# Early token loads, paired norms by log and exp, idle products and due times in an S4 and mixer kernel

## The chip, the cores and the metric

The kernel runs on one core of a Trainium2 chip. The metric is the device time of one execution in microseconds (us).

## The reference

The input `u` holds 2048 tokens of 512 features in f32. With xn = layernorm(u), the output is u + s * silu(b):

- `s` is an S4 layer: a convolution of every feature over the tokens with a kernel K of 2048 taps, plus xn * Dskip. K(d, l) is the real part of the sum over 128 states of C * dt * B * exp(dt * A * l). The convolution is computed by FFTs of length 4096.
- `b` is a mixer block with a norm of its own: x1 = xn + shift(gelu(layernorm(xn) @ w1)) @ w2, where the four quarters of the features are shifted by +1, -1, +2 and -2 tokens, and b = x1 + gelu(layernorm(x1) @ w3) @ w4, with 1376 hidden features.

```python
def _layernorm(x, axis=-1, eps=1e-5):
    m = jnp.mean(x, axis=axis, keepdims=True)
    v = jnp.var(x, axis=axis, keepdims=True)
    return (x - m) / jnp.sqrt(v + eps)
...
    x = A_u
    xn = _layernorm(x, axis=-1)
    s = _A_ref(xn, A_A_re, A_A_im, A_B_re, A_B_im, A_C_re, A_C_im, A_log_dt, A_Dskip)
    g = _silu(_B_ref(xn, B_w1, B_w2, B_w3, B_w4))
    return x + s * g
```

## The kernel before

**Tokens.** The 2048 tokens lie in the tile `X` as 16 steps of 128 tokens (the partitions) by 512 features. `loads()` brings everything in over the one DMA queue of SyncE (SP). `ln_first(q)` norms four steps at a time: statistics (`bn_stats`, `bn_aggr`) on VectorE (DVE), then `rstd`, a Sqrt on ScalarE (ACT) and a reciprocal on DVE, twice one after the other: `r1` for xn, and `r2` for the norm of xn, whose variance follows from `r1`. `h_pair(j)` transposes two normed steps on TensorE (PE) with `ident` (x2 to the bank pd, copied to `xT`), multiplies by w1 (bank pb) and takes the Gelu on ACT into `hT`. `u_stage1` multiplies the same steps by `ks1`, the first stage of the FFT (bank pa, copied to `ue` and written to the scratch `scr_Ud`).

**Shifts and second product.** `wrapped(k)` copies the shifted columns that cross a step into `hw` on DVE. `hs_pair` multiplies `hT` and `hw` by w2, adds into X and takes statistics. `ln_second` norms all 16 steps at once. `prep(jp)` splits w3 and w4 into two f16 halves each (`w3h`, `w4h`; a scale is a power of two that `pow2_scale` finds through a square root). `mlp(g)`, g from 0 to 7, computes two steps in f16 with three products for each (`x1T` by `w3h`, Gelu, `ghl` by `w4h`).

**The S4 kernel.** `params()` turns A, B, C and dt into logarithms, phases and magnitudes (`pn`, `tm`, then `par`). `tables(hf)` makes tables for eight chunks of 32 features, sixteen chunks `cc` in all: `block` the magnitudes `mag` for two chunks (64 exponentials of 128x64 on ACT, in groups of 16), `phases` and `remainders` the phases on DVE, `waves` the sines on ACT, `sums` the products of magnitudes and waves on DVE (`kt`, `pt`). PE contracts them over the states (bank pc, groups of 64 products for each chunk). `kstage1`, `products` (`uin`, `kin`, `pr`, `z1e`, through the scratch), `inverse` and `finish` are the FFT of the kernel, the product of spectra and the inverse; `gate` is the silu.

**The order.** No operation is issued where it is written. All are recorded by `Plan`, one list for PE, ACT, DVE and SP, and `Plan.order()` then runs a list scheduler over them: an engine takes, of the operations that are ready by the planner's own costs, the one with the least due time. The functions set this by `due(t)`, from constants (`H0`, `HC` for the tokens, `T0`, `TC` for the tables, `M0`, `MC` for the mixer and so on). An ACT function of another table than the loaded one (`TABLES`) adds `SWITCH` to the due time. An operation that may run on ACT or DVE (`E.copy`, `E.affine`) gets `PREFER` on DVE and `AVOID` on ACT:

```python
                    v = o.vt
                    if e == "ACT" and o.table and o.table != table:
                        v += SWITCH
                    if len(o.alts) > 1:
                        v += PREFER if e == "DVE" else AVOID
```

The order on every engine is thus fixed when the program is built; on the chip the engines run through their lists and wait for each other by semaphores. As all is issued from one place, every instruction of the profile has the line L279, and is told apart by its tiles. In the lists of before, the queue brings the tokens of steps 0 to 3 in two parts, the parameters between them, then w1, the other tokens and w2.

Of the kernel before, what the change touches and what calls it, by code (L numbers as in the profile page):

```python
# [83 lines left out]
class Op:  # L84
    __slots__ = (
        "eng", "alts", "calls", "cost", "deps", "succ", "table", "vt", "idx", "nbytes", "n", "ready", "start",
        "alias", "first", "last",
    )


TABLES = {
    AF.Exp: 1, AF.Sin: 2, AF.Arctan: 2, AF.Gelu_apprx_tanh: 3, AF.Sqrt: 4, AF.Silu: 5,
}
LATENCY = {"PE": 0.23, "ACT": 0.16, "DVE": 0.13, "SP": 0.0}
SAME = {"PE": 0.0, "ACT": 0.13, "DVE": 0.1, "SP": 0.0}
TABLE_LOAD = 1.41
DMA_RATE = 300e3
LAND, PAD = 3.32, 0.17
BASE, FINE, END = 16512, 19840, 229368

KGC = 3.25
SWITCH = 135.33
PREFER, AVOID = 290.89, 121.33
PV, T0, TC = 366.3, -80.6, 92.61
M0, MC, WC = 302.7, 225.43, 0.24
H0, HC, SC = -1212.9, 183.55, 0.09
KA, PA, PAC, FA = -108.1, -1278.7, 0.07, 1091.5
KB, PB, PBC, FB = -40.0, -299.0, 0.06, 186.2
FC = 0.16


def mlp_due(g, jp):
# [3 lines left out]
class Plan:  # L116
    def __init__(self, nc):
        self.engines = {"PE": nc.tensor, "ACT": nc.scalar, "DVE": nc.vector, "SP": nc.sync}
        self.ops = []
        self.cells = {}  # L120
        self.vt = 0.0
        self.group = None


# [33 lines left out]

    def new(self, table=0, nbytes=0):
        op = Op()  # L160
        op.alts, op.table, op.nbytes = {}, table, nbytes
        op.deps, op.alias, op.vt, op.idx = set(), set(), self.vt, len(self.ops)
        self.ops.append(op)
        return op


    def add(self, alts, writes, reads, table=0, nbytes=0):
        op = self.group or self.new(table, nbytes)
        for e, (cost, call) in alts.items():
            old = op.alts.setdefault(e, [0.0, []])  # L170
            old[0] += cost
            old[1].append(call)


        def after(other, name):
            if other[0] is not op:
                op.deps.add(other[0].idx)
                if other[1] != name:
                    op.alias.add(other[0].idx)

        for ap in reads:
            me = (op, ap.tensor.name)
            for c in self.cover(ap):
                if isinstance(c, str):
                    op.deps.update(self.cells[c])
                    continue
                st = self.cells.setdefault(c, [None, {}])
                if st[0] is not None:
                    after(st[0], me[1])
                if c[1] == "bank":  # L190
                    for r in st[1].values():
                        after(r, me[1])
                    st[0], st[1] = me, {}
                else:
                    st[1][op.idx] = me
        for ap in writes:
            me = (op, ap.tensor.name)
            for c in self.cover(ap):
                if isinstance(c, str):
                    self.cells.setdefault(c, []).append(op.idx)  # L200
                    continue
                st = self.cells.setdefault(c, [None, {}])
                if st[0] is not None:
                    after(st[0], me[1])
                for r in st[1].values():
                    after(r, me[1])
                st[0], st[1] = me, {}
# [12 lines left out]
    def order(self):  # L220
# [17 lines left out]
        while len(out) < len(ops):  # L238
# [4 lines left out]
            for o in pools[e]:  # L243
                if o.ready <= t + 0.02:
                    v = o.vt
                    if e == "ACT" and o.table and o.table != table:
                        v += SWITCH
                    if len(o.alts) > 1:
                        v += PREFER if e == "DVE" else AVOID
                    if pick is None or (v, o.idx) < score:  # L250
                        pick, score = o, (v, o.idx)
            for k in pick.alts:
# [136 lines left out]
def kernel(  # L389
# [54 lines left out]
    stats = keep([P, S, 6], "stats")  # L444
    mv = keep([P, S, 2], "mv")
    rs = keep([P, 4, S], "rs")
    bs = keep([P, S], "bs")
    wsc = keep([P, 16], "wsc")
    ssq = keep([P, 16], "ssq")
    ks1 = keep([P, 2 * NG], "ks1")  # L450
# [79 lines left out]
        turn["t"] += 1  # L530
        return bank[3][turn["t"] % 2]

    def rstd(dst, var):
        A.activation(dst, var, AF.Sqrt, bias=epst[:, 0:1], scale=1.0)
        V.reciprocal(dst, dst)

    def due(t):
        plan.vt = t


    def by_r(sb, dr, to_dram=False):
# [15 lines left out]
    raw = {"Ar": rawA[:, 0], "Ai": rawA[:, 1], "Br": rawC[:, 0], "Bi": rawC[:, 1], "Cr": rawC[:, 2], "Ci": rawC[:, 3]}  # L557

    def loads():
        due(0)  # L560
        by_r(X[:, 0:2], xv[:, :, 0:2])
        Q.dma_start(ev, c_ev)
        for n, src in (("Br", B_re), ("Cr", C_re), ("Bi", B_im), ("Ci", C_im), ("Ar", A_re), ("Ai", A_im)):
            Q.dma_start(raw[n], src.rearrange("(r p) n -> p r n", p=P))
        Q.dma_start(ld, log_dt.rearrange("(r p) -> p r", p=P))
        by_r(X[:, 2:4], xv[:, :, 2:4])
        load_w(w1, w1s, stile)
        Q.dma_start(ks1, c_ks1)
        for s0 in (4, 8, 12):
            by_r(X[:, s0 : s0 + 4], xv[:, :, s0 : s0 + 4])  # L570
        load_w(w2, w2s, w2place)
        Q.dma_start(is2, c_is2)
        V.memset(Dt, 0.0)
        for r in range(4):
            Q.dma_start(
                Dt[32 * r : 32 * r + 1], Dskip.rearrange("(h r m) -> r h m", h=2, r=4)[r].unsqueeze(0)
            )
# [58 lines left out]
    def block(blk):  # L636
# [23 lines left out]
            wmr[:, q0 : q0 + BQ].unsqueeze(1).to_broadcast([P, 4, BQ]),  # L660
        )
        for i in range(0, L2, 16):
            with plan.together(table=TABLES[AF.Exp]):
                for row in range(i, i + 16):
                    A.activation(mag[:, row], lgr[:, q0 : q0 + BQ], AF.Exp, scale=float(row))
        blocks[blk] = EB, pab, mag

    def phases(cc):

        if cc * CQ % BQ == 0:  # L670
            block(cc * CQ // BQ)
        EB, pab, mag = blocks[cc * CQ // BQ]
        q = cc * CQ
        sl = slice(q % BQ, q % BQ + CQ)
# [58 lines left out]

    def tables(hf):
        for cc in range(8 * hf, 8 * hf + 8):
            due(T0 + TC * cc)
            phases(cc)
            remainders(cc)
            waves(cc)
            sums(cc, factors(cc))  # L740


# [146 lines left out]
    def pow2_scale(cols, dst_s, dst_inv, target):  # L889
# [6 lines left out]
        A.activation(m1, m1, AF.Sqrt)  # L896
# [53 lines left out]
        w4t.append(w)  # L950


    def ln_first(q):
        ss = slice(4 * q, 4 * q + 4)
        for s in range(4 * q, 4 * q + 4):
            V.bn_stats(stats[:, s], X[:, s])
            V.bn_aggr(mv[:, s], stats[:, s])
        r1, r2, v = rs[:, 0, ss], rs[:, 1, ss], rs[:, 2, ss]
        rstd(r1, mv[:, ss, 1])
        V.tensor_mul(v, r1, r1)  # L960
        V.tensor_mul(v, v, mv[:, ss, 1])
        rstd(r2, v)
        V.scalar_tensor_tensor(bs[:, ss], mv[:, ss, 0], -1.0, r1, op0=ALU.mult, op1=ALU.mult)
        for s in range(4 * q, 4 * q + 4):
            E.affine(X[:, s], X[:, s], rs[:, 0, s : s + 1], bs[:, s : s + 1])

    hT = []

    def h_pair(j):
# [3 lines left out]
        for i in range(2):  # L973
            s = 2 * j + i
            x2 = wtile([P, D], F32, "x2")
            E.affine(x2, X[:, s], rs[:, 1, s : s + 1])
# [49 lines left out]
    def hs_pair(s0, k):  # L1026
# [11 lines left out]
        for i in range(2):  # L1038
            s = s0 + i
            V.tensor_add(X[:, s], X[:, s], acc[i])  # L1040
            V.bn_stats(stats[:, s], X[:, s])
            V.bn_aggr(mv[:, s], stats[:, s])

    def ln_second(ss):
        r3 = rs[:, 3, ss]
        rstd(r3, mv[:, ss, 1])
        V.tensor_scalar(r3, r3, XS, None, op0=ALU.mult)
        V.scalar_tensor_tensor(bs[:, ss], mv[:, ss, 0], -1.0, r3, op0=ALU.mult, op1=ALU.mult)


    x1Ts = {}
# [1 line left out]
    def mlp_input(g):  # L1053
# [3 lines left out]
        for i in range(2):  # L1057
            s = 2 * g + i
            xn = wtile([P, D], F32, "x1n")
            E.affine(xn, X[:, s], rs[:, 3, s : s + 1], bs[:, s : s + 1])  # L1060
            pt = t_bank() if g < 2 else mm_bank()
            with plan.together():
                for k in range(4):
# [48 lines left out]

    def token_mixing():
        V.memset(ssq, 0.0)
        for q in range(4):
            due(H0 + 2 * q * HC)
            ln_first(q)
            for j in (2 * q, 2 * q + 1):
                due(H0 + j * HC)
                h_pair(j)  # L1120
                u_stage1(2 * j)
                if j == 0:
                    for k in range(3, 6):
                        wrapped(k)
        for k in range(3):
            wrapped(k)
        for i in range(12):
            due(H0 + 2 * HC + i * 4.0)
            weight_squares(i)
        weight_scales()  # L1130
        due(H0 + 8 * HC)
# [65 lines left out]
```

## Time and profile before

| | |
|---|---|
| median of 3 runs | 680.08 us (679.99 to 680.60) |
| profiled execution | 679.28 us, its span 677.5 us |
| TensorE clock granted, mean | 0.981 |
| ACT table loads | 75, 96.2 us |
| DMA moved | 95.60 MB |

The span is the time between the first and the last instruction of the profiled execution; 1.78 us lie around it. Engines are PE (TensorE products), PEld (its weight loads, which run beside products), DVE, ACT, POOL and SP. A busy PE includes time in which a product is queued in the engine. A row of the timeline gives the start, the duration, the engine, the line, the operation, output<-input with the tiles' names, partitions x elements and count, and in brackets the idle time ahead of it and what ended that.

### The profile page before, as it was taken

The page shows a single profiled execution, that of the slowest core. Times are in us where ns is not written, and L with a number is a line of the kernel's source. Part 1 is how long each engine was busy: PE and PEld are TensorE (multiplying, and loading weights), DVE is VectorE, ACT ScalarE, POOL GpSimd, SP SyncE. Part 2 cuts the span into 40 slices and gives each one's busy share as a digit, 9 for nine tenths or more (in the row PEclk, how much of TensorE's full clock was granted, in tenths as well). Part 3 has the DMA queues.
Part 4 walks back from the last instruction along what each step waited for, and adds up shares of the span by engine and source line. Part 5 has one row for each costly group of instructions (what it writes and reads, how often), then busy time and mean ns, then how long its engine had stood idle before and what let it go on. Part 6 is the DMA issues. An engine that isn't in the chain of part 4 may idle for free.

```text
span 677.5 us, 13618 instructions
## 1 busy us (share of the span) xinstructions
PE 624.4 (92%) x5446; PEld 408.0 (60%) x5446; DVE 547.8 (81%) x783; ACT 459.2 (68%) x1020; POOL 0.7 (0%) x6
## 2 busy tenths in 40 slices
PE   0799999999996989899999999999999999999983
PEld 0376767666455667446768668657665756657541
DVE  4989789999999999999999989996344356465546
ACT  2889699998837999979989789883145342233220
POOL 0000000000000000000000000000000000000000
PEclk9999999899998999999999999999999999999995
DMA  9954442310111201365523342427389936642997
GB/s 245 247 196 141 150 158 102 98 71 20 66 63 49 78 33 48 70 159 155 155 72 110 102 122 83 140 74 196 104 239 346 255 89 193 163 149 78 263 333 229
DMA packets 100751, 95.60 MB, mean 141 GB/s; under 512 B 48656, under 2 KB 81424, under 8 KB 99792
## 3 DMA queue, kind: packets, MB, share of 16 engines
q1 hardware_dynamic: 100688, 94.73, 49.3%
q8 instruction: 43, 0.70, 0.4%
q14 instruction: 20, 0.16, 0.1%
HBM read 61.16 MB, written 33.55 MB: 140 GB/s over the span
## 4 chain that ended last, share of the span: by engine, by line
PE 46%; DVE 39%; ACT 6%; issue 5%; DMA 2%; SPq 1%; ACTq 0%
PE pb L279 16%; PE pa L279 13%; DVE pt L279 11%; PE pd L279 9%; DVE kt L279 8%; PE pc L279 7%; DVE X L279 4%; DVE pab L279 2%; DVE eg L279 2%; DVE stats L279 2%; ACT mag L279 2%; ACT L279 2%; DMA X<-in_A_u_dram 1%; DVE w4h L279 1%; DVE pr L279 1%
## 5 line engine op out<-in xcount | busy, mean ns | idle before, releaser
L279 PE MATMUL pa<-w4h,ghl 128*128 128x512 f16 (+1 forms) x528 | 123.9, 380 | 6.5 <-DVE ghl L279 5.6
L279 PE MATMUL pb<-x1T,w3h 128*128 128x256 f16 (+1 forms) x1056 | 124.2, 273 | 1.4 <-DVE x1T L279 1.2
L279 PEld LDWEIGHTS <-w3h 128*128 128x128 f16 (+1 forms) x1056 | 102.2, 100 | 27.9 <-issue 14.0
L279 ACT ACT_TABLE_LOAD x75 | 96.2, 1283 | 6.4 <-DMA wst<-in_B_w_dram 5.1
L279 PEld LDWEIGHTS <-ghl 128*128 128x128 f16 (+1 forms) x528 | 48.3, 98 | 74.8 <-issue 12.1
L279 ACT ACTIVATE mag<-par 128x64 f32<-128x64 f32 x512 | 83.8, 270 | 5.5 <-DVE kt L279 4.2
L279 PE MATMUL pc<-kt 128*32 128x64 f32 x1024 | 84.2, 416 | 2.7 <-DVE kev L279 1.4
L279 PE MATMUL pc<-pt 128*32 128x64 f32 x1024 | 78.1, 388 | 4.0 <-DVE pt L279 4.0
L279 ACT ACTIVATE g<-pb,wsc 128x512 f32<-128x512 f32 (+1 forms) x48 | 32.6, 690 | 64.0 <-PE pb L279 63.8
L279 PE MATMUL pb<-xT,w 128*128 128x256 f32 x256 | 59.8, 394 | 1.5 <-DVE xT L279 1.0
L279 PEld LDWEIGHTS pc<-pt 128*32 128x32 f32 x1024 | 56.3, 195 | 4.3 <-DVE pt L279 4.3
L279 PEld LDWEIGHTS pb<-xT,w 128*128 128x128 f32 x256 | 49.8, 197 | 14.8 <-DVE wsc L279 1.8
L279 PEld LDWEIGHTS pc<-kt 128*32 128x32 f32 x1024 | 48.6, 177 | 12.5 <-issue 9.5
L279 DVE SCALAR_TENSOR_TENSOR ghl<-g,wsc,ghl 128x512 f16<-128x512 f32 (+1 forms) x48 | 35.1, 744 | 23.8 <-ACT ghl L279 23.8
L279 DVE TENSOR_TENSOR pr<-pd,kh 128x512 f32<-128x512 f32 x48 | 33.6, 726 | 15.6 <-PE pd L279 15.3
L279 DVE TENSOR_TENSOR kt<-mag,kt 128x1024 f32<-128x1024 f32 x32 | 42.4, 1324 | 0.0
L279 DVE SCALAR_TENSOR_TENSOR pt<-kt,pt 128x2080 f32<-128x2080 f32 x16 | 38.9, 2429 | 0.8 <-ACT kt L279 0.7
L279 ACT ACTIVATE kt<-kt,halfpi 128x2080 f32<-128x2080 f32 x16 | 33.1, 2067 | 0.0
L279 ACT ACTIVATE pt<-pt 128x2080 f32<-128x2080 f32 x16 | 31.6, 1973 | 0.1
L279 ACT ACTIVATE ghl<-g,wsc 128x512 f16<-128x512 f32 (+1 forms) x43 | 30.6, 724 | 1.6 <-ACT g L279 0.9
L279 DVE BATCH_NORM_STATS2 stats<-X 128x6 f32<-128x512 f32 x32 | 22.0, 705 | 8.0 <-DMA X<-in_A_u_dram 7.5
L279 PE MATMUL pa<-w,hT 128*128 128x512 f32 x58 | 26.5, 597 | 0.0
(158 smaller groups left out, 920.7 us busy)
## 6 DMA issues: line engine op xcount, KB each, us to landing
wst<-in_B_w_dram SPq DMA_DIRECT2D x20, 512.0 KB, 3.9
scr_Ud<-ue SPq DMA_DIRECT2D x16, 512.0 KB, 3.2
scr_Kfa<-k1e SPq DMA_DIRECT2D x16, 256.0 KB, 3.8
uin<-scr_Ud SPq DMA_DIRECT2D x32, 128.0 KB, 3.1
cst<-c_gp SPq DMA_DIRECT2D x16, 256.0 KB, 2.8
kin<-scr_Kfa SPq DMA_DIRECT2D x32, 128.0 KB, 2.8
scr_Zda<-z1e SPq DMA_DIRECT2D x16, 256.0 KB, 2.7
xr<-in_A_u_dram SPq DMA_DIRECT2D x16, 256.0 KB, 7.6
```

Of the source, the lines that this page charges most:

```text
L279: ins = [getattr(self.engines[op.eng], name)(*args, **kw).ins for name, args, kw in op.calls]
```

## The change

- `loads()`: the queue's order has due times of its own (`LX`, `LC`, `LW`, `LP`, `LV`): the first tokens, w1 and `ks1`, the other tokens, then the parameters, w2 last.
- `rstd`: 1/sqrt(var + eps) is exp(-0.5 * ln(var + eps)) on ACT, and one Newton step of four small operations on DVE. `Ln` has the planner's table number of `Exp`. `pow2_scale` takes its square root by Ln and Exp as well.
- `ln_first`: both norms of a step are one call of `rstd` on a pair of variances (the second from var / (var + eps)), in slices of 2, 2, 4, 4 and 4 steps rather than four of 4.
- 36 products of `ident` by `ident` into a bank that nothing reads stand at the start, and an Exp on a column (`warm`).
- Each call of `due` is a stage of its own, to whose due time an entry of the list `SHIFT` (240 numbers) is added. Groups of magnitudes, phases and sums of one chunk have each their own.
- Operations that read PSUM get `PREFERP` and `AVOIDP` in place of `PREFER` and `AVOID`. All constants of due times are others, as are the planner's `LAND` (time of a DMA to land) and `PAD`.

```diff
-    AF.Exp: 1, AF.Sin: 2, AF.Arctan: 2, AF.Gelu_apprx_tanh: 3, AF.Sqrt: 4, AF.Silu: 5,
+    AF.Exp: 1, AF.Ln: 1, AF.Sin: 2, AF.Arctan: 2, AF.Gelu_apprx_tanh: 3, AF.Sqrt: 4, AF.Silu: 5,
...
-LAND, PAD = 3.32, 0.17
+LAND, PAD = 2.66, 0.13
...
-SWITCH = 135.33
-PREFER, AVOID = 290.89, 121.33
-PV, T0, TC = 366.3, -80.6, 92.61
-M0, MC, WC = 302.7, 225.43, 0.24
-H0, HC, SC = -1212.9, 183.55, 0.09
-KA, PA, PAC, FA = -108.1, -1278.7, 0.07, 1091.5
-KB, PB, PBC, FB = -40.0, -299.0, 0.06, 186.2
-FC = 0.16
+WARM = 36
+
+SHIFT = (
+    -3715, -2638, -688, 1005, -3173, -190, 267, 1280, 1181, 867, -512, -1077, 1355, 105, 2148, 920, 1539, 1545,
...
+)
+Q0, QC = 955.2, 0.12
+SWITCH = 4853.54
+PREFERP, AVOIDP = 3416.47, 1294.57
+PREFER, AVOID = 736.27, 6918.58
+PV, T0, TC = 1461.1, -148.8, 918.24
+LX, LC, LP, LW, LV = -4000.0, 0.11, -3268.4, -5077.4, -2984.5
+M0, MC, WC = 1956.5, 2587.23, 0.2
+H0, HC, SC = -1313.8, 567.49, 0.11
+KA, PA, PAC, FA = 775.7, -1535.4, 0.35, 1765.8
+KB, PB, PBC, FB = 1877.3, -190.5, 0.06, -1173.5
+FC = 0.23
...
                     if len(o.alts) > 1:
-                        v += PREFER if e == "DVE" else AVOID
+                        on = (PREFERP, AVOIDP) if o.psum else (PREFER, AVOID)
+                        v += on[e != "DVE"]
...
-    def rstd(dst, var):
-        A.activation(dst, var, AF.Sqrt, bias=epst[:, 0:1], scale=1.0)
-        V.reciprocal(dst, dst)
-
-    def due(t):
-        plan.vt = t
+
+    def rstd(dst, var, t, by=1.0):
+        A.activation(dst, var, AF.Ln, bias=epst[:, 0:1], scale=1.0)
+        A.activation(dst, dst, AF.Exp, scale=-0.5)
+        V.tensor_mul(t, dst, dst)
+        V.scalar_tensor_tensor(t, var, EPS, t, op0=ALU.add, op1=ALU.mult)
+        V.tensor_scalar(t, t, -0.5 * by, 1.5 * by, op0=ALU.mult, op1=ALU.add)
+        V.tensor_mul(dst, dst, t)
+
+    def due(t=None):
+        plan.stage += 1
+        t = plan.base = plan.base if t is None else t
+        plan.vt = t + (SHIFT[plan.stage] if plan.stage < len(SHIFT) else 0)
...
     def loads():
-        due(0)
+        due(LX)
         by_r(X[:, 0:2], xv[:, :, 0:2])
+        due(LW)
+        load_w(w1, w1s, stile)
+        Q.dma_start(ks1, c_ks1)
+        due(LP)
         Q.dma_start(ev, c_ev)
...
-        by_r(X[:, 2:4], xv[:, :, 2:4])
-        load_w(w1, w1s, stile)
-        Q.dma_start(ks1, c_ks1)
-        for s0 in (4, 8, 12):
-            by_r(X[:, s0 : s0 + 4], xv[:, :, s0 : s0 + 4])
+        for k, (s0, s1) in enumerate(((2, 4), (4, 8), (8, 12), (12, 16))):
+            due(LX + LC * (k + 1))
+            by_r(X[:, s0:s1], xv[:, :, s0:s1])
+        due(LV)
         load_w(w2, w2s, w2place)
...
         for i in range(0, L2, 16):
+            due()
             with plan.together(table=TABLES[AF.Exp]):
...
+    def ln_first(ss):
+        steps = range(ss.start, ss.stop)
+        for s in steps:
+            V.bn_stats(stats[:, s % 8], X[:, s])
+            V.bn_aggr(mv[:, s, 0:2], stats[:, s % 8])
+        var, t = mv[:, ss, 1], tn[:, ss, 0]
+        V.tensor_scalar(t, var, EPS, None, op0=ALU.add)
+        V.reciprocal(t, t)
+        V.tensor_mul(mv[:, ss, 2], var, t)
+        rstd(r12[:, ss], mv[:, ss, 1:3], tn[:, ss])
+        V.scalar_tensor_tensor(bs[:, ss], mv[:, ss, 0], -1.0, r12[:, ss, 0], op0=ALU.mult, op1=ALU.mult)
+        for s in steps:
+            E.affine(X[:, s], X[:, s], r12[:, s, 0:1], bs[:, s : s + 1])
...
+        for j in range(8):
+            due(H0 + j * HC)
+            if j in (0, 1, 2, 4, 6):
+                ln_first(slice(2 * j, 2 * j + (2 if j < 2 else 4)))
+            h_pair(j)
+            u_stage1(2 * j)
...
+    due(LX)
     V.memset(halfpi, float(np.pi / 2))
+    A.activation(warm, halfpi, AF.Exp)
+
+    with plan.together(cost=10.0):
+        for k in range(WARM):
+            T.matmul(bank[0][0][:, :P], ident, ident, start=True, stop=True)
```

More of the change, by code (lines that the diff above doesn't have):

```diff
@@ L86 @@
         "eng", "alts", "calls", "cost", "deps", "succ", "table", "vt", "idx", "nbytes", "n", "ready", "start",
-        "alias", "first", "last",
+        "alias", "first", "last", "psum",
     )
 TABLES = {
-    AF.Exp: 1, AF.Sin: 2, AF.Arctan: 2, AF.Gelu_apprx_tanh: 3, AF.Sqrt: 4, AF.Silu: 5,
+    AF.Exp: 1, AF.Ln: 1, AF.Sin: 2, AF.Arctan: 2, AF.Gelu_apprx_tanh: 3, AF.Sqrt: 4, AF.Silu: 5,
 }
@@ L121, in __init__ @@
         self.vt = 0.0
+        self.stage, self.base = -1, 0.0
         self.group = None
@@ L160, in new @@
         op = Op()
-        op.alts, op.table, op.nbytes = {}, table, nbytes
+        op.alts, op.table, op.nbytes, op.psum = {}, table, nbytes, False
         op.deps, op.alias, op.vt, op.idx = set(), set(), self.vt, len(self.ops)
@@ L168, in add @@
         op = self.group or self.new(table, nbytes)
+        op.psum = "PSUM" in str(reads[0].space) if reads else False
         for e, (cost, call) in alts.items():
@@ L443 @@
     ones = keep([1, P], "ones")
-    stats = keep([P, S, 6], "stats")
-    mv = keep([P, S, 2], "mv")
-    rs = keep([P, 4, S], "rs")
+    stats = keep([P, 8, 6], "stats")
+    mv = keep([P, S, 3], "mv")
+    r12 = keep([P, S, 2], "rs")
+    r3 = keep([P, S], "rs")
+    tn = keep([P, S, 2], "rs")
     bs = keep([P, S], "bs")
+    warm = keep([P, 1], "warm")
     wsc = keep([P, 16], "wsc")
@@ L668, in phases @@
     def phases(cc):
-        if cc * CQ % BQ == 0:
-            block(cc * CQ // BQ)
         EB, pab, mag = blocks[cc * CQ // BQ]
@@ L735, in tables @@
         for cc in range(8 * hf, 8 * hf + 8):
+            if cc * CQ % BQ == 0:
+                due(T0 + TC * cc)
+                block(cc * CQ // BQ)
             due(T0 + TC * cc)
@@ L738, in tables @@
             remainders(cc)
+            due(T0 + TC * cc)
             waves(cc)
+            due(T0 + TC * cc)
             sums(cc, factors(cc))
@@ L895, in pow2_scale @@
         V.tensor_scalar(m1, m1, 1e-34, 1e34, op0=ALU.max, op1=ALU.min)
-        A.activation(m1, m1, AF.Sqrt)
+        A.activation(m1, m1, AF.Ln)
+        A.activation(m1, m1, AF.Exp, scale=0.5)
         T.matmul(pt[:, P : P + 1], ones, m1, start=True, stop=True)
@@ L950, in prep @@
         w4t.append(w)
[L953 to L965, printed above, removed]
+    def ln_first(ss):
[11 more added lines that the diff above has]
+            E.affine(X[:, s], X[:, s], r12[:, s, 0:1], bs[:, s : s + 1])
     hT = []
@@ L975, in h_pair @@
             x2 = wtile([P, D], F32, "x2")
-            E.affine(x2, X[:, s], rs[:, 1, s : s + 1])
+            E.affine(x2, X[:, s], r12[:, s, 1:2])
             pt = t_bank()
@@ L1040, in hs_pair @@
             V.tensor_add(X[:, s], X[:, s], acc[i])
-            V.bn_stats(stats[:, s], X[:, s])
-            V.bn_aggr(mv[:, s], stats[:, s])
+            V.bn_stats(stats[:, s % 8], X[:, s])
+            V.bn_aggr(mv[:, s, 0:2], stats[:, s % 8])
     def ln_second(ss):
[L1045 to L1048, printed above, removed]
+        rstd(r3[:, ss], mv[:, ss, 1], tn[:, ss, 0], XS)
+        V.scalar_tensor_tensor(bs[:, ss], mv[:, ss, 0], -1.0, r3[:, ss], op0=ALU.mult, op1=ALU.mult)
     x1Ts = {}
@@ L1059, in mlp_input @@
             xn = wtile([P, D], F32, "x1n")
-            E.affine(xn, X[:, s], rs[:, 3, s : s + 1], bs[:, s : s + 1])
+            E.affine(xn, X[:, s], r3[:, s : s + 1], bs[:, s : s + 1])
             pt = t_bank() if g < 2 else mm_bank()
@@ L1114, in token_mixing @@
         V.memset(ssq, 0.0)
[L1115 to L1124, printed above, removed]
+        for j in range(8):
[4 more added lines that the diff above has]
+            u_stage1(2 * j)
+            if j == 0:
+                for k in range(3, 6):
+                    wrapped(k)
         for k in range(3):
@@ L1127, in token_mixing @@
         for i in range(12):
-            due(H0 + 2 * HC + i * 4.0)
+            due(Q0 + QC * i)
             weight_squares(i)
```

13 rows, old and new, of the table SHIFT are left out of this document.

## The prediction

> **What bounds the kernel now.** I read the page first for which engine is full when, then the busy times by stage, then the places where one engine holds another.
>
> ```profile
> span 677.5 us, 13618 instructions
> PE 624.4 (92%) x5446; PEld 408.0 (60%) x5446; DVE 547.8 (81%) x783; ACT 459.2 (68%) x1020; POOL 0.7 (0%) x6
> ...
> PE   0799999999996989899999999999999999999983
> ...
> DVE  4989789999999999999999989996344356465546
> ACT  2889699998837999979989789883145342233220
> ```
>
> PE at 92% says little by itself: VectorE (DVE) reads 9 from slice 7 to 27 but for one 8, and both DVE and ScalarE (ACT) have air only behind that. By stage (columns: length, then busy time of PE, PEld, DVE, ACT, POOL with counts, the granted PE clock, DMA share, GB/s):
>
> ```profile
> 0.00:31.84 31.84, 10.64 (x40) 4.60 (x40) 21.82 (x48) 17.97 (x51) 0.70 (x6) 1.00 1.01 247
> 31.84:102.00 70.16, 68.06 (x355) 50.31 (x352) 61.68 (x123) 61.77 (x121) 0.00 (x0) 1.00 0.50 165
> 102.00:204.00 102.00, 100.18 (x793) 62.10 (x795) 101.87 (x144) 84.19 (x216) 0.00 (x0) 0.98 0.20 68
> 204.00:336.00 132.00, 117.18 (x1264) 82.09 (x1255) 131.90 (x141) 122.57 (x303) 0.00 (x0) 0.97 0.35 94
> 336.00:461.00 125.00, 124.18 (x1252) 83.74 (x1252) 120.56 (x150) 106.66 (x238) 0.00 (x0) 1.00 0.36 103
> 473.00:656.70 183.70, 183.70 (x1524) 113.59 (x1524) 89.44 (x149) 59.91 (x88) 0.00 (x0) 1.00 0.71 197
> 656.70:677.50 20.80, 8.41 (x113) 2.40 (x112) 14.97 (x25) 1.06 (x1) 0.00 (x0) 0.62 0.85 254
> ```
>
> Three regimes: a start in which all wait for tokens; 102 to 461, where DVE is busy 354.3 of 359 us; and a PE stage without a gap from there to 656.7, with a tail behind it. The handover from DVE to PE is the last place where PE waits for DVE:
>
> ```profile
> 444.71 0.74 DVE L279 COPY z1e<-pd 128x256 f32<-128x256 f32 x2
> ...
> 445.18 1.08 PE L279 MATMUL pd<-kin,cst 128*64 128x256 f32 x8
> ```
> ```profile
> 0.00:130.52 130.52, 105.40 (x716) 76.73 (x716) 111.96 (x208) 108.09 (x266) 0.70 (x6) 0.99 0.58 170
> ...
> 0.00:138.22 138.22, 113.10 (x740) 79.89 (x740) 119.66 (x219) 115.73 (x273) 0.70 (x6) 0.99 0.56 167
> ...
> 0.00:445.12 445.12, 404.36 (x3532) 273.43 (x3532) 421.98 (x582) 383.24 (x913) 0.70 (x6) 0.99 0.39 112
> ```
>
> The copy of z1e ends at 445.12, the product that reads it starts at 445.18. DVE had then worked 421.98 us and idled 23.1, of which 18.6 (130.52 - 111.96) lay before 130.52 and 4.5 behind. From 445.18 the program needs 232.3 us more (677.5 - 445.18). So the time of the profiled execution is 422.0 of DVE work + 23.1 of DVE idle + 0.1 + 232.3 + 1.8 around the span (679.28 - 677.5) = 679.3; it stands 0.8 below the median of 680.08. What decides is each of three terms: how much DVE work stands ahead of the last hold, how much PE work is left behind it, and how long DVE idles, which it does in the first 130 us.
>
> **Work that is moved.** Counting both built programs' instructions in their order on each engine, each at the mean duration of its kind in this trace: the DVE work ahead of the copy that holds PE last is 421.1 before and 422.2 after (after, it is a copy of pr), +1.1. The PE work ahead of the product held is 386.0 before and 395.9 after, and PE has 0.3 less to do up to its last table group: 9.9 + 0.3 = 10.2 us of products move from behind the hold to ahead of it, where PE idled anyway. This is the change's real gain: in the profile PE has slack before 445 and none after, so 232.3 becomes 222.1. Behind the last product of the final stage DVE has 13.5 us of work instead of 14.6: -1.1 in the tail. So
>
> time = (422.0 + 1.1) + idle of DVE + 0.1 + 222.1 - 1.1 + 1.8 = 646.0 + idle.
>
> With the 23.1 of before this would be 669.1; equal times need 33.3. All else hangs on DVE's idle time, and so on the start.
>
> **The start.** The rows of the first pair:
>
> ```profile
> 7.47 1.28 DVE L279 BATCH_NORM_STATS2 stats<-X 128x6 f32<-128x512 f32 x2 [6.23 <-DMA X<-in_A_u_dram]
> ...
> 15.63 1.29 DVE L279 BATCH_NORM_STATS2 stats<-X 128x6 f32<-128x512 f32 x2 [1.29 <-DMA X<-in_A_u_dram]
> ...
> 21.29 2.42 PE L279 MATMUL pa<-X,ks 32*64 32x512 f32 x8 [1.45 <-DVE X L279]
> ...
> 28.03 1.97 PE L279 MATMUL pd<-ident,x 128*128 128x128 f32 x8 [1.18 <-DVE x L279]
> ...
> 31.84 9.76 PE L279 MATMUL pb<-xT,w 128*128 128x256 f32 x32
> ...
> 41.44 1.04 PE L279 MATMUL pd<-ident,x 128*128 128x128 f32 x8
> 43.51 7.14 PE L279 MATMUL pb<-xT,w 128*128 128x256 f32 x32 [1.04 <-DVE xT L279]
> 50.59 1.09 PE L279 MATMUL pa<-X,ks 32*64 32x512 f32 x8
> ```
>
> Today the first norm waits for four steps of tokens, whose second half comes behind the parameters: statistics end at 16.9, the first w1 product starts 14.9 later, at 31.84. With a norm of two steps it hangs on the first arrival alone, statistics ending at 8.75. The same 14.9 would put the product at 23.7; the two affine steps that are no longer ahead take off a little, three table loads in the norms put some back; I take 22.5 to 23.7, some 8 to 9 us earlier.
>
> ```profile
> L279 ACT ACT_TABLE_LOAD x75 | 96.2, 1283 | 6.4 <-DMA wst<-in_B_w_dram 5.1
> ...
> L279 ACT ACTIVATE rs<-mv,epst 128x4 f32<-128x4 f32 x4 | 1.2, 294 | 0.5 <-DVE mv L279 0.3
> ...
> L279 DVE TENSOR_TENSOR rs<-rs 128x4 f32<-128x4 f32 x4 | 0.6, 156 | 0.0
> ```
>
> The norms: Sqrt becomes Ln and Exp. The built program has a table load ahead of each Ln and another ahead of the Exp behind it, so the planner's one number for both saves nothing: loads go from 75 to 79, by 1283 ns 5.1 us of ACT. Four Newton operations of 0.156 for a reciprocal are 0.5 us of DVE a norm, but computing both norms at once halves their count and drops two products, so that it comes to nothing. The Trainium skill says otherwise: "ScalarE: Activation LUTs", section "Table sets: the hidden batching unit", has one set that holds both ln and exp, so that ln followed by exp is one load. This trace has no Ln; what that would make of the time is a rival below.
>
> The idle products: 36 of some 0.25 us (1.97 / 8) are 9 us; from about 1.5 us they last to 10.5. The first real products come at about 16, with the first norm of 14.1 (behind the statistics and their small steps at 9.1, four small activations of 0.294 and three loads of 1.283) and its affine steps. Cold against warm costs 9.76 - 7.14, 1.97 - 1.04 and 2.42 - 1.09, 4.9 us together in the rows above. Does a gap of 5.5 us make PE cold again? The nearest row:
>
> ```profile
> 115.50:119.00 3.50, 2.11 (x35) 1.76 (x33) 3.50 (x4) 3.50 (x17) 0.00 (x0) 1.00 0.06 21
> 119.00:122.40 3.40, 3.40 (x57) 2.26 (x49) 3.40 (x5) 3.40 (x22) 0.00 (x0) 0.50 0.34 95
> ```
>
> 3.5 us with PE busy 60% were followed by 3.4 at clock 0.50, so I take it that 5.5 empty ones do the same, and give the idle products nothing; if the clock stayed up, the first product would end up to 2.6 earlier. The Trainium skill's "TensorE: Matmul & The Clock Gate", section "Part 1: The HAM clock gate (the "warmup" mystery)", speaks against this part too: half rate again after one idle window of about 3.4 us. By it the sum stands as it is; with the clock kept up it would be 2.6 lower.
>
> **What the earlier start meets.** ACT. Its order in the changed program puts 19.3 us of work ahead of the second Gelu of the first pair, which needs that product's end: 22.5 + 9.8 = 32.3, or 29.6 warm. So ACT idles 10.3 to 13.0 there. The parameters now come behind 5 MB of tokens and w1; at the 247 GB/s of the first row by stage they land at about 25 to 31, so DVE's work on them, for which the table exponentials wait, is late too: those wait for a ratio that itself waits for ACT, another 2.1 us in the order. I take 14 us of idle ACT.
>
> ```profile
> L279 DVE COPY ue<-pa 128x512 f32<-128x512 f32 x17 | 11.4, 688 | 3.8 <-PE pa L279 3.7
> ...
> L279 ACT COPY ue<-pa 128x512 f32<-128x512 f32 x15 | 8.8, 613 | 1.3 <-PE pa L279 1.2
> ```
>
> From there ACT has no air. The split between ACT and DVE changes: of the copies, these among them, ACT gets 130 after 107, and DVE 100 after 123. Up to the last Gelu behind w1 ACT has 118.9 us of work, before 116.8 (27 table loads among it, before 26). DVE's work ahead of the copies that wait for this Gelu falls from 110.9 to 102.7.
>
> ```profile
> 130.52 0.23 DVE L279 COPY hw<-hT 128x96 f32<-128x96 f32 x1
> ...
> 137.62 0.60 ACT L279 ACTIVATE hT<-pb 128x512 f32<-128x512 f32 x1
> ```
>
> Today the Gelu ends at 138.22 with 115.73 of ACT work, and DVE isn't held by it. After, it ends at 115.73 + 2.1 + 14.3 = 132.1, earlier than today by 6. But DVE stands at the copies with 103.7 behind it (the count is 1.0 under the row of 0 to 130.52), so it has idled 28.4, 9.8 more than the 18.6 of today. Everything behind those copies in DVE's fixed order waits, the sums of the tables first, for which PE's groups wait. Two waits come on top. The conversion of w3 has again 16.2 us more ACT work ahead of it than DVE work ahead of its reader, and by then ACT has idled 2.4 more, waiting for PE: 2.4. The second norm's Ln and Exp with a load of 1.283 between stand where one Sqrt stood: 1.283 + 0.294 + 0.13 = 1.7. Behind that, DVE and PE hand to each other with little to spare in both kernels: 4.5 today; the lead of DVE's work over PE's grows by less after, and I take 3.0 (bounds 0 and 4.5).
>
> Idle = 28.4 + 2.4 + 1.7 + 3.0 = 35.5, time 646.0 + 35.5 = 681.5 against 679.28. That is +2.2, and on the median of 680.08 it is 682.3. The gain of 10.2 behind the hold is paid by 12.4 of idle DVE.
>
> **The rivals.** *The start's lead is kept (faster).* ACT waits 10 instead of 14 (a warm clock in the first product, no wait for the parameters), and DVE loses nothing more than the 2.4: idle 28.4 - 4 + 2.4 = 26.8, so 672.8, to 669.1 with the idle of before. For it: the first product is earlier by 8 to 9 us, and ACT had 22.5 us of idle time up to the last Gelu (138.22 - 115.73) that shrinks in any case. Against it: the clock, and the handing over, which costs 4.5 today.
>
> *The start's lead is lost (slower still).* The late parameters hold ACT for as long as today, 22.5 us instead of 14.3: everything behind moves by 8.2, idle 43.7, 689.7. It decides where the parameters' chain on DVE ends later than 32 us, the time of the first Gelus. For it: the loads of tokens keep the queues full to 25 us and more. Against: by then ACT has the Gelus of the second pair.
>
> *It doesn't do what it says for the tables.* One load for Ln and Exp: six of the 27 loads ahead of the last Gelu go, 7.7 us, and the time is 681.5 - 7.7 = 673.8. This is what the Trainium skill's section on table sets above would give. The built program names two different sets for the two functions, so I give it 3 in 100.
>
> **How the numbers follow.** The forecast has 0.45; its own range, with idle from 32 to 40, is 678 to 686 in the profiled execution, 678.8 to 686.8 on the median. The lead kept has 0.39, lost 0.13, one load 0.03. What a measurement of this kernel can tell from no change is about 0.2%, 1.4 us, so 678.7 to 681.4 is the same: 0.12 of the forecast's 0.45, the other 0.33 lie above. Faster: 0.39 + 0.03 = 0.42; same 0.12; slower 0.33 + 0.13 = 0.46. The range is 669 (the lead kept in full, idle as before) to 692 (lead lost, 689.7 and the 0.8 to the median, with 1.5 for the 4.5 of handing over instead of 3.0); it leaves out some 5 in 100 below, and 6 above.
>
> **What would show it.** Right: first w1 product at about 23 and clock 0.5 in it; two table loads to each norm; the last Gelu at about 132 with DVE waiting for ACT just ahead of a copy of hw; DVE idle of about 35 up to the last hold; then PE without a gap for 222 us to the end. Wrong: if DVE's idle time at that point is below 30, the start was mis-sized; if the stretch behind the hold isn't some 10 us shorter, the moved products were.

## The result and the profile after

The changed kernel takes 685.26 us (median of 8 runs, 682.24 to 686.90) against 679.71 us (8 runs beside it): a ratio of 1.0081, 95% interval 1.0063 to 1.0098. It is slower by 5.5 us; 682.3 was forecast, with a range of 669 to 692. The profiled execution took 685.73 us. The page of the changed kernel, in the lines that were shown of before:

```profile
span 683.9 us, 13816 instructions
...
PE 639.9 (94%) x5518; PEld 422.5 (62%) x5518; DVE 544.7 (80%) x794; ACT 472.4 (69%) x1041; POOL 0.7 (0%) x6
...
PE   6996999798899699999899999999999999999993
...
DVE  4778799799899999999999998999514356465557
ACT  5798899898956899979998978996415443233220
```

PE is now busy from the first slice, with the idle products and an earlier first pair. DVE, which read 9 nearly throughout from slice 7, still has a 7 in slice 8 (120 to 137 us) and an 8 in slice 11: it waits longer at the start. The stages, in busy time:

```profile
31.84:102.00 70.16, 63.64 (x325) 45.82 (x324) 57.52 (x105) 65.49 (x149) 0.00 (x0) 0.90 0.41 137
102.00:204.00 102.00, 92.81 (x768) 58.34 (x767) 95.84 (x130) 87.74 (x220) 0.00 (x0) 0.97 0.26 86
...
0.00:137.37 137.37, 120.22 (x782) 91.28 (x783) 106.23 (x216) 117.83 (x282) 0.70 (x6) 0.89 0.50 147
...
0.00:442.37 442.37, 409.22 (x3524) 280.47 (x3525) 403.65 (x580) 379.41 (x911) 0.70 (x6) 0.96 0.39 112
442.41:683.90 241.49, 230.72 (x1994) 141.98 (x1993) 141.06 (x215) 92.92 (x132) 0.00 (x0) 0.98 0.69 191
```

Up to 137.37 DVE has idled 31.1 us (137.37 - 106.23); before it was 18.6 up to 130.52. Up to the last hold it is 38.7 (442.37 - 403.65) against 23.1. PE is granted 0.90 of its clock between 32 and 102 us, where it was 1.00. (The column doesn't show every slow stretch: in the kernel before it reads 1.00 also over the first w1 product, which took 9.76 us where the next took 7.14.) The places of the argument, in the timeline:

```profile
22.70 9.17 PE L303 MATMUL pb<-xT,w 128*128 128x256 f32 x32
...
132.87 0.30 DVE L303 COPY hw<-hT 128x96 f32<-128x96 f32 x2 [0.96 <-ACT hT L303]
...
136.39 0.60 ACT L303 ACTIVATE hT<-pb 128x512 f32<-128x512 f32 x1 [0.84 <-PE pb L303]
...
137.02 0.51 DVE L303 COPY hw<-hT 128x96 f32<-128x96 f32 x4 [2.70 <-ACT hT L303]
...
442.41 1.47 PE L303 MATMUL pb<-x1T,w3h 128*128 128x256 f16 x12 [0.73 <-DVE x1T L303]
```

The first w1 product starts 9.1 us earlier than before (22.70 against 31.84), but the last Gelu behind w1 ends at 136.99, 1.2 earlier. The last wait of PE for DVE ahead of the tail is at 442.41, for `x1T`; 241.5 us lie behind it.

The time can be told from there: the last hold ends at 442.4; 442.4 + 241.5 + 1.8 around the span = 685.7. In all variants below that share this order the stretch behind that hold is 241.5 to 242.8 us, so that their times are told by one number, the moment of the hold.

### The profile page after: what moved, and what is told of

It reads as the page before. It is cut to its first block, busy times and chain, and to the rows that moved or that the text cites. A ratio compares the mean times of both kernels' runs of the same rounds, so it can differ in the third digit from the quotient of the medians.

```text
span 683.9 us, 13816 instructions
## 1 busy us (share of the span) xinstructions
PE 639.9 (94%) x5518; PEld 422.5 (62%) x5518; DVE 544.7 (80%) x794; ACT 472.4 (69%) x1041; POOL 0.7 (0%) x6
## 5 line engine op out<-in xcount | busy, mean ns | idle before, releaser
L303 PE MATMUL pb<-x1T,w3h 128*128 128x256 f16 (+1 forms) x1056 | 126.4, 276 | 2.0 <-DVE w3h L303 1.3
L303 PE MATMUL pa<-w4h,ghl 128*128 128x512 f16 (+1 forms) x528 | 121.4, 380 | 0.6 <-DVE ghl L303 0.3
L303 PE MATMUL pb<-xT,w 128*128 128x256 f32 x256 | 64.8, 414 | 0.0
L303 PEld LDWEIGHTS pb<-xT,w 128*128 128x128 f32 x256 | 52.5, 209 | 14.4 <-issue 3.2
L303 ACT ACTIVATE ghl<-g,wsc 128x512 f16<-128x512 f32 (+1 forms) x37 | 26.0, 705 | 38.2 <-PE pa L303 36.4
L303 DVE TENSOR_TENSOR pr<-pd,kh 128x512 f32<-128x512 f32 x48 | 34.3, 740 | 13.3 <-PE pd L303 12.5
L303 ACT ACTIVATE pt<-pt 128x2080 f32<-128x2080 f32 x16 | 31.1, 1941 | 0.2
L303 PE MATMUL pb<-w,hT 128*128 128x512 f32 x58 | 26.2, 596 | 1.7 <-DVE X L303 1.7
L303 ACT ACTIVATE kt<-pt 128x2080 f32<-128x2080 f32 x11 | 21.3, 1935 | 9.2 <-DVE pt L303 9.2
```

The costliest lines, as they stand in the source:

```text
L303: ins = [getattr(self.engines[op.eng], name)(*args, **kw).ins for name, args, kw in op.calls]
```

## Experiments

The variants of the changed kernel keep the order of every engine's list but for what they name; single operations were replaced, or moved once the planner had made the order, so that no new schedule is mixed in. All were timed beside the kernel before (679.1 to 679.6 us).

### One table load for two functions

This variant computes other numbers than the norm; it is there for its time alone.

```diff
-        A.activation(dst, var, AF.Ln, bias=epst[:, 0:1], scale=1.0)
+        A.activation(dst, var, AF.Exp, bias=epst[:, 0:1], scale=1.0)
...
-        A.activation(m1, m1, AF.Ln)
+        A.activation(m1, m1, AF.Exp)
```

> The changed kernel with Exp in the place of each Ln (norms and scales come out as other numbers; the lists of all engines stay the same but for table loads: 16 of 79 fall away, 12 of them ahead of the last Gelu behind w1, 15.4 us of ScalarE). Theory (ScalarE is what bounds the first 137 us, and its lead over VectorE turns into idle VectorE): the last Gelu comes 9 to 14 us earlier, VectorE's idle time up to 442 falls from 38.7 to 25 to 29, and the time falls by 9 to 13, to about 674. Rival (the loads are hidden and the time comes from the order of PE and VectorE behind 150 us): the time stays within 2 us of 685.

Measured: 672.36 us, ratio 0.9910 (0.9897 to 0.9923). That is 12.9 below the changed kernel. In the groups of the changed kernel, then of this one:

```profile
L303 ACT ACT_TABLE_LOAD x79 | 101.4, 1283 | 2.1 <-PEq L1231 0.7
```
```profile
L303 ACT ACT_TABLE_LOAD x63 | 80.8, 1283 | 1.8 <-PEq L1231 0.7
```

The timeline of this variant, and its busy time up to the last hold:

```profile
16.95 7.17 PE L303 MATMUL pb<-xT,w 128*128 128x256 f32 x32
...
124.85 0.63 ACT L303 ACTIVATE hT<-pb 128x512 f32<-128x512 f32 x1
...
429.08 1.47 PE L303 MATMUL pb<-x1T,w3h 128*128 128x256 f16 x12 [0.61 <-DVE x1T L303]
```
```profile
0.00:429.05 429.05, 403.12 (x3524) 276.91 (x3525) 402.59 (x580) 357.81 (x894) 0.70 (x6) 0.97 0.40 116
```

The last Gelu comes 11.5 us earlier, the hold 13.3, and DVE idles 26.5 instead of 38.7. The rival falls: of the 15.4 us of the 12 loads that are gone ahead of that Gelu, 12.9 come off the time. The loads act in part through the clock: with a shorter norm the first w1 product starts at 16.95 and takes 7.17 us instead of 9.17.

### Sqrt again, in the changed order

```diff
         A.activation(dst, var, AF.Ln, bias=epst[:, 0:1], scale=1.0)
+        plan.ops[-1].swap = "ACT", [("activation", (dst, var, AF.Sqrt), {"bias": epst[:, 0:1], "scale": 1.0})]
         A.activation(dst, dst, AF.Exp, scale=-0.5)
+        plan.ops[-1].swap = "DVE", [("reciprocal", (dst, dst), {})]
...
         A.activation(m1, m1, AF.Ln)
+        plan.ops[-1].swap = "ACT", [("activation", (m1, m1, AF.Sqrt), {})]
         A.activation(m1, m1, AF.Exp, scale=0.5)
+        plan.ops[-1].swap = "ACT", []
```

Once the order is made, an operation's `swap` takes its place; an empty one drops the operation.

> The changed kernel with the norms and the two scales by Sqrt again (norms still in pairs, reciprocal on VectorE behind it, the Newton step kept; 70 table loads instead of 79, 7 of the 9 ahead of the last Gelu behind w1; all lists else the same). Theory (each load ahead of the last Gelu counts, as 12 fewer were worth 13 us): 7 x 1.28 = 9 us less on ScalarE, time lower by 6 to 9, 676 to 679, about the kernel before. Rival (only the loads of the scale, at 121 to 126, hold PE; those of the norms are hidden): lower by 0 to 3, since one of the two loads ahead of that scale stays.

Measured: 676.06 us, ratio 0.9941 (0.9925 to 0.9957): 9.2 below the changed kernel, and 3.5 below the kernel before. In its timeline:

```profile
14.17 1.09 PE L311 MATMUL pa<-X,ks 32*64 32x512 f32 x8 [1.88 <-issue]
...
128.46 0.63 ACT L311 ACTIVATE hT<-pb 128x512 f32<-128x512 f32 x1
...
432.86 1.47 PE L311 MATMUL pb<-x1T,w3h 128*128 128x256 f16 x12 [0.58 <-DVE x1T L311]
```

Seven loads ahead of the last Gelu are 9.0 us, and the hold comes 9.5 earlier. Ln and Exp in norms and scales alone thus turn the change from a gain into a loss. The wait ahead of the first product here is 1.88 us behind the idle products, and it runs at full clock (1.09 us for eight products against 2.43 in the changed kernel).

### The idle products, with and without the long norm

In the changed kernel, and in the Sqrt variant:

```diff
-WARM = 36
+WARM = 1
```

> The changed kernel with 1 idle product instead of 36. Theory (the clock is down again before the first real product, so the idle products do nothing): first w1 product still about 9.2 us long and starting at 22.7, time within 1 us of the changed kernel. Rival (they keep part of the clock up): the products up to 32 us get longer and the time rises by 1 to 3 us.

> The Sqrt variant with 1 idle product at the start instead of 36. There the first real products come at 14.2, some 2 us behind the last idle one, and run at full clock (7.2 us for the first w1 product against 9.2 in the changed kernel). Theory (idle products pay only where the norm behind them is short enough): without them the first product takes 9 to 10 us, time higher by 1 to 3. Rival (idle products never matter): first product as long, time within 1 us.

Measured: in the changed kernel 686.71 us, ratio 1.0106 (1.0091 to 1.0121), 1.5 above 685.26 with overlapping intervals; in the Sqrt variant 677.79, ratio 0.9981 (0.9969 to 0.9993), 1.7 above 676.06 with intervals apart. The first w1 product, of the first and the second:

```profile
21.77 9.83 PE L303 MATMUL pb<-xT,w 128*128 128x256 f32 x32
```
```profile
18.39 9.92 PE L311 MATMUL pb<-xT,w 128*128 128x256 f32 x32
```

In the changed kernel it was 9.17 long and ended at 31.87, here it is longer, starts earlier and ends at 31.60: the idle products bring nothing at that place. The theory's "within 1 us" was missed by 0.5, on the rival's side; as the intervals overlap, whether the 1.5 is more than noise stays open.

In the Sqrt variant the product was 7.17 long and ended at 24.40, here it is 9.92 long and ends at 28.31: the idle products do keep the clock there. The times differ by 1.7 us, but the trace doesn't show that this comes from the early clock. The last Gelu and the hold without idle products:

```profile
127.56 0.63 ACT L311 ACTIVATE hT<-pb 128x512 f32<-128x512 f32 x1
...
432.91 1.47 PE L311 MATMUL pb<-x1T,w3h 128*128 128x256 f16 x12 [0.70 <-DVE x1T L311]
```

The Gelu is 0.9 us earlier than with them (128.46), and the hold stands where it stood (432.86). So in the two profiled executions nothing of the 3.9 us at the first product reaches the hold, and what the idle products are worth stays open. In the changed kernel the first real product comes 4.5 us behind them, and the clock is down:

```profile
16.53 2.43 PE L303 MATMUL pa<-X,ks 32*64 32x512 f32 x8 [4.54 <-DVE X L303]
```

### Idle products where PE stands still

24 products of `ident` are put ahead of the transposes that wait at 59.3, 14 ahead of the product that waits for the scale at 126.4, both into banks that are written next.

```diff
+        for (op, dst), n in (((turns[8], turns[8].calls[0][1][0]), 24), (first[0], 14)):
+            op.calls = [("matmul", (dst, self.ident, self.ident), {"start": True, "stop": True})] * n + op.calls
```

> The changed kernel with idle products added at two places where PE stands still: 24 ahead of the transposes at 59.3 and 14 ahead of the product at 126.4. Theory (two stretches at half clock, 59 to 71 and 122 to 136, lengthen the chain PE to ScalarE, about 4 us together in the waits of ScalarE for PE): clock 1.0 there, last Gelu 3 to 4 us earlier, time lower by 2 to 4. Rival (PE is not on the path there): clock 1.0, time within 1 us.

Measured: 682.17 us, ratio 1.0046 (1.0033 to 1.0058), 3.1 below the changed kernel. The changed kernel there, as timeline and as busy time:

```profile
59.34 1.97 PE L303 MATMUL pd<-ident,x 128*128 128x128 f32 x8 [5.98 <-DVE x L303]
...
126.39 0.58 PE L303 MATMUL pd<-m,ones 1*128 1x1 f32 x2 [3.49 <-ACT m L303]
126.90 6.51 PE L303 MATMUL pb<-xT,w 128*128 128x256 f32 x16
```
```profile
61.00:71.00 10.00, 10.00 (x36) 5.41 (x35) 8.12 (x20) 9.87 (x15) 0.00 (x0) 0.50 0.51 173
```

The variant:

```profile
51.00:61.00 10.00, 9.57 (x75) 6.95 (x73) 9.96 (x26) 8.14 (x48) 0.00 (x0) 1.00 0.01 2
61.00:71.00 10.00, 8.28 (x34) 5.38 (x32) 7.65 (x20) 9.88 (x14) 0.00 (x0) 0.83 0.59 205
```
```profile
132.36 0.63 ACT L315 ACTIVATE hT<-pb 128x512 f32<-128x512 f32 x1
```

Behind two gaps of 6.0 and 3.5 us the changed kernel's products run at half clock; with idle products in the gaps the last Gelu comes 4.0 us earlier. The rival falls. The theory's "clock 1.0" was met only in part: the clock is 0.83 between 61 and 71 us, where it fell again although no gap there is longer than 0.9 us. The Trainium skill, "TensorE: Matmul & The Clock Gate", section "Part 1: The HAM clock gate (the "warmup" mystery)", sets the limit at one idle window of about 3.4 us. The two gaps of the changed kernel agree with it, and so does the 1.88 us that kept the clock; other gaps here don't. The second pair of the Sqrt variant, and of the last variant below:

```profile
28.98 0.66 PE L311 MATMUL pd<-ident,x 128*128 128x128 f32 x4 [2.69 <-ACT xT L311]
29.47 7.17 PE L311 MATMUL pb<-xT,w 128*128 128x256 f32 x32
```
```profile
26.91 0.66 PE L319 MATMUL pd<-ident,x 128*128 128x128 f32 x4 [2.46 <-ACT xT L319]
27.41 8.86 PE L319 MATMUL pb<-xT,w 128*128 128x256 f32 x32
```

A gap of 2.69 us kept the clock, one of 2.46 lost it: the granted clock is 0.50 from 28 to 31 us there. In the Sqrt variant a gap of 1.81 us at 148 lost it too (0.50 between 151 and 152 us). So by these traces the length of one gap alone doesn't decide; what else does stays open.

### Copies from ScalarE to VectorE

```diff
+        early = [
+            op for op in out
+            if op.eng == "ACT" and op.calls[0][0] == "copy" and op.calls[0][1][0].tensor.name.split("_")[0] in ("ue", "xT", "par")
+        ]
+        for op in early[18:31]:
+            op.eng, op.calls = "DVE", op.alts["DVE"][1]
```

> The changed kernel with 13 copies out of PSUM, which ScalarE makes between 60 and 107 us, moved to VectorE at their places in the order (7.5 us off ScalarE, 8.5 onto VectorE, all other lists the same). Theory (ScalarE has 16 us more work ahead of the last Gelu than VectorE): the last Gelu comes 4 to 7 us earlier, VectorE idles 10 to 14 us less up to the copies of hw, and the time falls by 3 to 6, to 679 to 682. Rival (VectorE is the bound as a whole, its work counts wherever it stands): the time rises by 5 to 8.

Measured: 686.88 us, ratio 1.0112 (1.0095 to 1.0129): neither. The theory said lower by 3 to 6, the rival higher by 5 to 8; it is 1.6 above the changed kernel. The timeline of this variant, and its busy time from 98 to 134 us, show why the sum of ScalarE's work was the wrong measure:

```profile
117.09 5.83 ACT L312 ACTIVATE mag<-par 128x64 f32<-128x64 f32 x32 [1.40 <-DVE pt L312]
...
128.34 0.38 PE L312 MATMUL pd<-m,ones 1*128 1x1 f32 x2 [2.72 <-ACT m L312]
...
137.03 0.60 ACT L312 ACTIVATE hT<-pb 128x512 f32<-128x512 f32 x1 [0.84 <-PE pb L312]
```

```profile
98.00:134.30 36.30, 32.66 (x343) 26.72 (x347) 36.04 (x44) 31.65 (x100) 0.00 (x0) 0.91 0.31 109
```

DVE is busy 36.04 of the 36.30 us, where it was 34.20 in the changed kernel; with more copies in its list it frees `pt` later, ACT's exponentials wait 1.40 us for that, the scale `m` behind them comes 2 us later, PE waits 2.72 us for the scale and goes on at a clock of 0.56 (128.34 to 131 us), and the last Gelu stands where it stood. The path up to the last Gelu goes from engine to engine, and ACT's list is only part of it: table loads lie on it, while copies between 60 and 107 us that move to DVE bring nothing.

### The order of the loads

In the changed kernel the DMA queue of before; and in the kernel before, the tokens of steps 2 and 3 ahead of the parameters.

```diff
+        first = [op for op in out if op.eng == "SP"][:31]
+        new = first[:4] + first[23:31] + first[4:8] + first[8:23]
...
+        first = [op for op in out if op.eng == "SP"][:17]
+        out = first[:4] + first[13:17] + first[4:13] + [op for op in out if op not in first]
```

> The changed kernel with the DMA queue in the order of the kernel before (tokens of steps 0 and 1, parameters, tokens of steps 2 and 3, w1, other tokens); all other lists as they are. Theory (early tokens start the first product 8 to 9 us earlier, and the start is on the path): the second norm waits for tokens at 15.6, the first w1 product starts at 29 to 31, time higher by 5 to 8. Rival (the earlier start is lost in the waits behind it anyway): higher by less than 2.

> The kernel before with the tokens of steps 2 and 3 ahead of the parameters in the DMA queue, all else the same. Theory (an early load pays only if the lists of the engines ask for it early: VectorE's list of before has six operations on the parameters ahead of the statistics of steps 2 and 3): the first w1 product starts within 1.5 us of 31.8 and the time is the same or up to 2 us higher. Rival (the load order by itself is worth the 7 us that its undoing cost in the changed kernel): first product at 24 to 26, time lower by 4 to 7.

Measured: the changed kernel with the old queue 692.63 us, ratio 1.0188 (1.0171 to 1.0205), 7.4 above the changed kernel; the kernel before with early tokens 680.42, ratio 1.0017 (1.0006 to 1.0027). First products of the one and the other:

```profile
29.37 6.91 PE L309 MATMUL pb<-xT,w 128*128 128x256 f32 x25
```
```profile
32.67 7.64 PE L284 MATMUL pb<-xT,w 128*128 128x256 f32 x22
```

The early tokens are worth 7 us in the changed kernel and nothing in the old one, whose DVE list has work on the parameters ahead of the second pair of statistics: these start at 16.47 there, behind operations on `rawC`, though their tokens now stand ahead of the parameters in the queue (15.63 in the kernel before). Load order and list go together.

### All that helps

Reciprocal roots by bits on DVE with idle products; the same with seven copies moved; and Sqrt without the Newton step, with 26 idle products at 55 us.

```diff
+            ("tensor_scalar", (bits, var.bitcast(I32), 1, None), {"op0": ALU.logical_shift_right}),
+            ("tensor_scalar", (bits, bits, -1.0, 1597463174.0), {"op0": ALU.mult, "op1": ALU.add}),
...
+        for op in early[18:25]:
...
+        turns[8].calls = [idle] * 26 + turns[8].calls
```

> The changed kernel with both suspects taken away in a way that keeps the output: reciprocal square roots from a shift of the bits and two Newton steps on VectorE (63 table loads, 40 more small operations on VectorE, 28 of them early where it idles), and the idle products at 59 and 126 us. Theory: last Gelu at 121 to 126, idle VectorE up to the last hold of 24 to 27, time 670 to 675, below both kernels; behind the last hold 241 us as in the changed kernel. Rival (small operations on VectorE cost as much as loads on ScalarE): 678 to 682.

> As the one before, and the first 7 of the 13 copies of the copy experiment (those between 60 and 87 us, where VectorE still had idle time) on VectorE. Theory (a copy is free where VectorE waits, and costs where it is full): 1 to 3 us lower than without them. Rival (what counts is the chain from engine to engine, not ScalarE's sum of work): within 1 us, or higher.

> The Sqrt variant of the changed kernel, without the Newton step behind Sqrt and reciprocal (23 small operations on VectorE fewer), and with 26 idle products ahead of the transposes at 55 us, where PE stands still for 6.4 us and then runs at half clock. Theory (the early chain over ScalarE, VectorE and PE counts up to the last Gelu): clock 1.0 from 55 to 65, last Gelu 1 to 4 us earlier than the 128.5 of the Sqrt variant, time lower by 1 to 4, 672 to 675. Rival (neither is on the path any more): within 1 us of 676.

Measured: 675.20 us, ratio 0.9933 (0.9914 to 0.9953); 676.34, ratio 0.9948 (0.9936 to 0.9961); 673.38, ratio 0.9923 (0.9901 to 0.9945). The first is 0.2 us above the theory's range: its ScalarE has as few loads as the first experiment, and DVE idles 22.3 us up to the hold (24 to 27 foretold), but 40 more small operations on DVE raise its work up to there from 402.59 to 408.88. The copies bring nothing again. The third is the fastest of those that compute the norms: 5.9 us below the kernel before, as timed beside it (679.31), and 11.9 below the changed one. The last Gelu comes at 125.30, 3.8 us earlier than in the Sqrt variant, and the clock is 1.0 from 51 to 71 us, as foretold; but its interval overlaps with that of the Sqrt variant, so that the 2.7 us between their times aren't clear of noise. Its last hold:

```profile
426.71 1.47 PE L319 MATMUL pb<-x1T,w3h 128*128 128x256 f16 x12 [0.71 <-DVE x1T L319]
```

The profiled execution is the fastest of its six (670.63).

## Why the prediction was right

The direction and the mechanism held: the order behind 150 us was a gain, idle DVE at the start more than paid for it. The size was too small: +2.2 us forecast, +5.5 measured, the small rest of two terms of opposite sign; the idle time of 38.7 lies in the 32 to 40 that the forecast took for itself. The gain of the order is read from the sum; no run takes it by itself. The steps:

- **The sum's constant.** Predicted: time = 646.0 + idle of DVE for the profiled execution. In the trace: 403.65 of DVE work + 38.7 + 241.5 + 1.8 = 685.7, so a constant of 647.0. At another idle time it holds too: 402.6 + 26.5 + 241.5 + 1.8 = 672.4 in the first experiment. With the 23.1 of before the changed order would take 670.1 against 679.28: the gain of the moved products is 9.2, predicted 10.2. The hold is another one than foretold: `x1T`, and the 241.5 us behind it are longer than the 232.3 of before, not 10 shorter. The sum holds all the same, as DVE and PE are both busy all the 21.09 us from there to 463.50, about where the foretold `pr` is done and DVE has worked 425.0 us (423.1 in the sum). From the product that reads this `pr`, at 464.43, 219.5 us are left, against 221.0 in the sum.
- **Idle DVE.** Predicted 28.4 up to the copies of `hw`, 35.5 up to the hold; measured 31.1 and 38.7. What it adds behind the copies, 7.1, came out at 7.6, with some luck: the wait for w3, put at 2.4, is 2.0 (at 174.32), the second norm's, put at 1.7, is 0.8 (at 229.09), and the other waits make 4.8 against 3.0. The term that was too small is the last Gelu, put at 132.1 and seen ending at 136.99.
- **That Gelu.** The first product at 22.5 to 23.7 was right (22.70, 9.17 long, cold at first: 0.53 granted from there to 27). ACT's idle time was put at 14, and at 14.3 in the sum; it is 12.8 at 42.57 (42.57 - 29.82), and 1.8 more for `tm` at 53.69 make 14.6. But it is 19.5 at the last Gelu (136.99 - 117.45): 4.6 us of waits for PE came on top, which the sum had left out, though it had shown a row at half clock behind a gap. Idle products in those gaps brought the Gelu to 132.99, 0.9 from the forecast, and the time to 682.17, against 682.3 forecast. This is the step that was mis-sized, and the experiment gives its size: 3.1 us.
- **ScalarE as the bound.** Right for its table loads, wrong as a sum of work: 7.5 us of copies taken off it and put on DVE brought nothing.
- **The rival of one load.** Priced at 6 loads, 7.7 us and 673.8; the order without Ln has 12 fewer ahead of the Gelu, since the load back to Exp falls away with each, and took 672.4. Why it isn't so in the built program: Ln and Exp are loaded from two sets. The timeline of the changed kernel:

```profile
9.63 0.30 ACT L303 ACTIVATE rs<-mv,epst 128x4 f32<-128x4 f32 x1 [6.12 <-DVE mv L303]
...
9.95 1.28 ACT L303 ACT_TABLE_LOAD   x1
...
11.24 0.21 ACT L303 ACTIVATE rs<-rs 128x4 f32<-128x4 f32 x1
11.47 1.28 ACT L303 ACT_TABLE_LOAD   x1
```

  The Trainium skill, "ScalarE: Activation LUTs", section "Table sets: the hidden batching unit", has one load for the two. These rows differ: a load stands between the Ln and its Exp, and the next behind it.
- **The idle products.** "Give them nothing" was right for this kernel within 1.5 us. The reason given holds too: behind the gap of 4.5 us the products run cold, and with a shorter norm they don't, though nothing of that is seen at the hold.
- **The two rivals of the start.** Neither decided: ACT's wait was not the 10 of the lead kept. The late parameters were seen as foretold (exponentials waiting 1.83 us for `tm` at 53.69), and did not hold ACT for 22 us.

## What to carry to other kernels

Look up in the built program which functions share a table load before giving them one number in a planner: the wrong guess put loads around every norm and cost 9 us here, more than the early tokens brought. An early load pays only if the lists of the engines ask for it early, and idle products keep the clock only if the real ones follow soon; whether the end of the kernel moves with it has to be seen at the last hold. Where three engines hand a chain around, a sum of one engine's work doesn't tell the time; take off the work that lies on the chain.

## What was not expected of the hardware

The clock of TensorE was a cost well behind the start: two gaps of 6.0 and 3.5 us at 53 and 123 us, and half clock behind each, took 3 us of the whole time. Gaps of 2.5 us and less could lose the clock as well, and one of 2.69 us could keep it. The times of the changed order spread more than those of before (682.24 to 686.90 against 678.54 to 680.60 in 8 runs each; the best variant 670.63 to 676.33 in 6); where this comes from stays open.
